# Products of v_m and w1 for four batches at once, kept in memory: an attention and mixture-of-experts kernel on one core

## The chip, the cores and the metric

The kernel runs on one core of one Trainium2 chip. The metric is the device time of one execution in microseconds; for the kernel before it is 1374.86 us, the median of 3 runs (1374.76 to 1375.8). A profile is one further execution, taken by the hardware profiler. In it the engines are PE (matmuls; PEld loads their weights), DVE (vector), ACT (scalar), POOL (GpSimd) and SP, which here only issues DMAs.

## The reference

Two parts, one behind the other, all in 32-bit floats. The first is an attention with 32 learned memory slots per head (8 batches, 8 heads, 576 positions, 64 per head); the second sends its result through four experts, weighted by given probabilities:

```python
a = softmax(phi, over positions)                    # 8 x 8 x 576 x 32
k_m, v_m = einsum(a, k), einsum(a, v)               # 32 slots of 64, per batch and head
attn = softmax(q @ k_m.T / 8, over the slots)
x = (attn @ v_m), heads side by side                # 4608 rows of 512
for e in range(4):
    h = maximum(x @ w1[e], 0.0)                     # 512 -> 1024
    out += p[:, e:e + 1] * (h @ w2[e])              # 1024 -> 512
```

## The kernel before

x is never formed. Since x = attn @ v_m, x @ w1 is attn @ (v_m @ w1): per batch, expert and half of the 1024 hidden columns the kernel makes a product of v_m and w1 ("vw": 2 tiles of 128 rows, 4 heads by 32 slots each, by 512 columns) and multiplies the transposed attention weights (AT) with it. 32-bit accuracy comes from pairs: a tile is split into a high part (a copy that rounds, on ACT) and a rest (a subtraction, on DVE or POOL), and PE does high x high, high x rest and rest x high.

**Tiling and order.** Batches go in four groups of two (odd is 0 or 1). A group has 4 experts, an expert 32 steps (STEPS), a group 128 (PAIR). Up to BEGIN, in the middle of group 1, the first stage runs step by step: `first` makes a tile of h, `second` multiplies it with w2 (lines 490 to 538). From BEGIN on the second stage runs in 80 units of 4 steps (`unit`, line 874); a unit does a block of h times w2 with seven block products (`product`, L819: a11, a12, t2, t3, t1, n4, a22) instead of eight, with operands that DVE, ACT and POOL make a unit ahead out of `rows` (L733 to L735). Four units are one block of weights; `load_part` (L682) fetches its 8 tiles (kw, plain w2, and v, precomputed sums of w2, both kept in memory), three of them in the first three units of the block before and five in its last, as buffers come free.

**What sets the order around the change.** The plan is a table written out by hand: `at(s, ...)` puts a piece of work at a step, and `run_plan` emits it where that step stands in the unit. All engines run their own instructions in order, SP its DMAs too: a DMA that waits for a buffer holds those behind it. ATT, VW_AT, VW_7, W1_AT, W1_7 and JOBS are those tables: when a batch's phi, k_m and v_m, scores and transposes are done, when a vw product is made, when w1 is loaded, when the sums of w2 are made and stored.

**vw in the kernel before.** `vw_mm` (L462) makes one product for one batch, expert and half: 8 matmuls with 64 rows by 32 columns against 512, each into its own 32 rows of two PSUM banks. `vw_out` copies the high part (ACT, L476) and subtracts (DVE, L477). The w1 tiles are loaded by `load_w1` (L166) into four buffers, which the matmuls free. In the second stage one of the four, and one of the five vw1 buffers, belongs to the ring of block weights. Only PSUM banks 0 and 1 are then free for the attention's and the vw's matmuls.

The prologue (lines 938 to 993) is written out by hand for batch 0; `keep_warm` (L935) is a run of matmuls without use.

Of the kernel before, what the change touches and what calls it, by code (L numbers as in the profile page):

```python
# [38 lines left out]

W1_AT = (15, 16, 17, 18)  # L40
VW_AT = (
    ((20, 23), (28, 33)),
    ((20, 23), (28, 32)),
    ((20, 23), (26, 31)),
    ((18, 28), (26, 33)),
    ((20, 23), (28, 30)),
    ((17, 20), (23, 26)),
)

ATT = {  # L50
    2: (22, 30, (93, 97, 102), (111, 112, 113)),
    3: (38, 46, (116, 118, 120), (PAIR + 2, PAIR + 4, PAIR + 6)),
    4: (88, 99, (PAIR + 66, PAIR + 76, PAIR + 84), (PAIR + 86, PAIR + 89, PAIR + 95)),
    5: (107, PAIR - 2, (PAIR + 102, PAIR + 108, PAIR + 115), (PAIR + 118, PAIR + 124, PAIR + 128)),
    6: (PAIR + 3, PAIR + 14, (2 * PAIR + 66, 2 * PAIR + 76, 2 * PAIR + 84), (2 * PAIR + 86, 2 * PAIR + 89, 2 * PAIR + 95)),
    7: (PAIR + 18, PAIR + 32, (2 * PAIR + 102, 2 * PAIR + 108, 2 * PAIR + 115), (2 * PAIR + 118, 2 * PAIR + 124, 2 * PAIR + 128)),
}

REST_0 = (2, 1, 6, 6, 1, 1, 5)
# [6 lines left out]
Q = 256  # L66
X_BANK, Y_BANK, AB_BANK = 4, 2, 6
JOBS = (
    (2, 0, 18, "Y", 5), (2, 1, 34, "Y", 5), (3, 0, 85, "Y", 5), (3, 1, 98, "Y", 5),
    (0, 0, PAIR + 2, "Y", 5), (0, 1, PAIR + 16, "Y", 5), (1, 0, PAIR + 30, "Y", 5),  # L70
    (1, 1, PAIR + 44, "Y", 5),
)
KEEP_AT, W2_AGAIN = (20, 12, -1, 20), 24
FIRST_LOADS = (-16, -7, -6, -5, -4, -3, -2, -1)
W1_7 = (6, 7, 22, 23)
VW_7 = (
    ((17, 34), (28, 36)),
    ((16, 35), (30, 38)),
    ((14, 30), (18, 34)),
    ((14, 30), (18, 38)),  # L80
    ((17, 34), (28, 36)),
    ((16, 35), (30, 38)),
    ((14, 30), (18, 34)),
    ((14, 30), (18, 34)),
    ((14, 30), (18, 34)),
)


@with_exitstack
def body(ctx: ExitStack, tc: tile.TileContext, qm, qt, kv, kvt, phi, prob, w1, w2, out):  # L90
# [238 lines left out]
    def kv_pick(b, gs=range(2), copy=nc.scalar.copy):  # L329
        src = st["kvp", b, gs[0]]  # L330
        n = 2 * len(gs)
        copy(
            kvm[b][:, 2 * gs[0]:2 * gs[0] + n].rearrange("p a j m -> p (a j m)"),
            src.rearrange("p g m -> p (g m)"),
        )
        give(src)
# [27 lines left out]

# [91 lines left out]
    def vw_mm(b, e, fh):  # L456

        ps = [bank("pm", 512) for _ in range(2)]
        for hp in range(NP):
            for j in range(2):  # L460
                r, m = v_half(j), slice(M * hp, M * hp + M)
                nc.tensor.matmul(  # L462
                    ps[j][m], kvm[b][r, hp, j], w1t[e, fh, hp // 2][r, hp % 2], start=True, stop=True
                )
# [8 lines left out]
    def vw_out(ps, b, e, fh, js=(0, 1)):  # L473
        for j in js:
            t = vw_tile(b // 2, e, b % 2, fh, j)
            nc.scalar.copy(t[:, 0, :], ps[j])  # L476
            nc.vector.tensor_sub(t[:, 1, :], ps[j], t[:, 0, :].bitcast(F32))  # L477
            give(ps[j])
# [85 lines left out]
    def at(s, unit):  # L564
        plan[s].append(unit if isinstance(unit, tuple) else (None, unit))
# [28 lines left out]
    def attention(b, s, turn, scores, turns):  # L594

        at(s, lambda: load_phi(b))
        at(turn, lambda: load_tail(b))
        for g in range(2):
            at(s + 3, lambda g=g: phi_max(b, g))
            at(s + 4, lambda g=g: phi_exp(b, g))  # L600
            at(s + 5, lambda g=g: phi_norm(b, g))
            at(turn + g, lambda g=g: phi_turn(b, g))
            at(turn + 1 + g, lambda g=g: phi_turn_out(b, g))
        at(turn + 2, lambda: phi_turn_tail(b))
        at(turn + 3, lambda: phi_turn_tail_out(b))
# [4 lines left out]
        at(turn + 12, lambda: kv_fold(b))  # L610
        at(turn + 13, lambda: kv_pick(b))
# [12 lines left out]
    for k in range(NG):  # L624
        for e in range(E):
# [69 lines left out]
    ph2 = {}  # L695

    def open_seven():
        two = lambda tag, n, *names: [
            att.tile([P, 2, 2, n], F32R, name=tag, tag=tag, bufs=2) for _ in range(2)
        ]  # L700
        ph2["Y"] = two("Y", Q)
        ph2["D"] = [
            t.rearrange("p s t (j c) -> p s t j c", j=2) for t in two("D", Q)
        ]
        ph2["N"] = two("N", P)
        for tag, n in ("g", 3), ("d", 2):
            ph2[tag] = att.tile([P, n, 2, P], F32, name=tag, tag=tag)
        ph2["n"] = att.tile([P, 2, P], F32, name="n", tag="n")
# [230 lines left out]
    with tc.manual_schedule():  # L939
# [27 lines left out]
        for g in range(2):
            for c2 in range(2):
                kv_mm(0, g, c2, raw["kv", 0, g, c2])
            kv_out(0, g)  # L970
            kv_fold(0, range(g, g + 1))
            kv_pick(0, range(g, g + 1), dve.tensor_copy)
# [12 lines left out]
        transposes_out(0, 0)
        keep_warm(4)
        for i in range(2):
            split_w2(0, 0, i, raw["w2", 0, 0], gps)
        for s in range(AHEAD):
            first(s)  # L990
# [12 lines left out]
    with tc.manual_schedule():  # L1003
# [59 lines left out]
```

## Time and profile before

| | |
|---|---|
| median of 3 runs | 1374.86 us |
| profiled execution, time | 1374.65 us |
| its span, first to last instruction | 1372.9 us |
| mean granted TensorE clock | 0.992 |
| PE busy | 1340.4 us (98%) |
| DVE, ACT, POOL busy | 769.5, 481.8, 396.6 us |
| DMA | 220.41 MB, mean 161 GB/s |
| second stage begins at | 568.6 us (its unit 0) |
| groups 2 and 3 begin at | 732.6 and 1061.0 us (units 16 and 48) |

How to read the rows. A group of instructions stands as line, engine, operation, what it writes <- what it reads, shapes and count, then busy time in us and mean ns of one, then idle time of the engine ahead of it and what ended that. A row of the waits is who waited <- for whom: us in total, times, longest us. A timeline row is start us, length us, then the instruction, with idle time ahead of it in brackets; neighbours of one kind are merged, and "SPq" is SP issuing. A matmul's length is longer than its distance to the next one, since they are pipelined: what a matmul costs PE is the distance from start to start.

### The profile page before, as it was taken

The numbers are of one execution on the slowest core, as the hardware profiler recorded it, in microseconds if no ns is written. First come the engines' busy times: TensorE is split into PE (matmuls) and PEld (weight loads), VectorE is DVE, ScalarE is ACT, GpSimd is POOL, SyncE is SP. The second block draws the span as 40 slices with busy tenths as digits, with TensorE's granted clock in tenths as the row PEclk, the third lists the DMA queues.
The fourth block names the chain that finished last, engine by engine and source line by source line (L and its number), as shares of the span: only waits on it lengthen the run. The fifth ranks groups of instructions, "written<-read, shape, count | busy, mean of one in ns | idle before, by whom it ended". The sixth has DMA issues, their size and how long they took to land.

```text
span 1372.9 us, 26361 instructions
## 1 busy us (share of the span) xinstructions
PE 1340.4 (98%) x10306; PEld 1170.6 (85%) x10306; DVE 769.5 (56%) x1798; ACT 481.8 (35%) x1215; POOL 396.6 (29%) x452
## 2 busy tenths in 40 slices
PE   7999999999999999999998999999999999999998
PEld 5687888878788787889887999988889899999998
DVE  4654423255343534566675666666666566666665
ACT  4433323243232332333333333333333333333332
POOL 1020304054002222243332333334343233333332
PEclk8999999999999999999999999999999999999999
DMA  8751827038565762633325533343522444443321
GB/s 307 254 200 62 301 93 262 32 119 300 185 235 203 250 213 86 215 112 114 143 102 208 188 119 120 116 151 112 200 93 97 188 154 154 154 154 133 127 94 72
DMA packets 64845, 220.41 MB, mean 161 GB/s; under 512 B 7249, under 2 KB 8401, under 8 KB 64721
## 3 DMA queue, kind: packets, MB, share of 16 engines
q1 hardware_dynamic: 55504, 185.17, 38.8%
q0 software_dynamic: 8064, 29.36, 5.4%
q10 hardware_dynamic: 1152, 4.19, 0.8%
q8 instruction: 81, 1.33, 0.4%
q14 instruction: 44, 0.35, 0.1%
HBM read 175.71 MB, written 42.99 MB: 159 GB/s over the span
## 4 chain that ended last, share of the span: by engine, by line
PE 93%; DVE 3%; DMA 2%; ACT 1%; issue 1%; SPq 0%; DVEq 0%; ACTq 0%
PE banks L819 29%; PE banks L534 7%; PE banks L535 7%; PE banks L536 7%; PE banks L733 6%; PE banks L735 6%; PE banks L734 6%; PE banks L462 5%; PE banks L501 4%; PE banks L502 4%; PE banks L503 4%; PE banks L857 1%; PE banks L858 1%; PE banks L859 1%; PE banks L307 1%; DVE vw L477 1%
## 5 line engine op out<-in xcount | busy, mean ns | idle before, releaser
L837 DVE SCALAR_TENSOR_TENSOR acc<-banks,pt,acc 128x256 f32<-128x256 f32 x528 | 252.1, 480 | 183.6 <-PE banks L819 182.1
L733 PE MATMUL banks<-AT,vw 128*128 128x256 f32 (+1 forms) x640 | 191.1, 299 | 0.0
L735 PE MATMUL banks<-AT,vw 128*128 128x256 f32 (+1 forms) x640 | 190.4, 298 | 0.0
L734 PE MATMUL banks<-AT,vw 128*128 128x256 f32 (+1 forms) x640 | 190.1, 297 | 0.0
L515 DVE SCALAR_TENSOR_TENSOR h<-banks,h 128x256 fp32r<-128x256 f32 x192 | 80.3, 420 | 170.7 <-ACT h L513 111.1
L800 POOL TENSOR_TENSOR D<-d,D 128x512 fp32r<-128x512 f32 x80 | 103.6, 1295 | 225.6 <-ACT D L799 162.7
L534 PE MATMUL banks<-w,h 128*128 128x512 f32 x384 | 151.3, 394 | 0.6 <-ACT h L513 0.6
L535 PE MATMUL banks<-w,h 128*128 128x512 f32 x384 | 150.9, 393 | 0.0
L536 PE MATMUL banks<-w,h 128*128 128x512 f32 x384 | 150.4, 392 | 0.0
L819 PE MATMUL banks<-w,Y 128*128 128x256 f32 x912 | 136.4, 284 | 7.0 <-DMA w<-kw 7.0
L513 ACT ACTIVATE h<-banks 128x256 fp32r<-128x256 f32 x192 | 73.4, 384 | 186.1 <-PE banks L503 157.2
L819 PEld LDWEIGHTS banks<-w,Y 128*128 128x128 f32 x912 | 123.6, 190 | 11.3 <-DMA w<-kw 3.9
L205 POOL TENSOR_TENSOR raw<-raw,sv 128x512 fp32r<-128x512 f32 x32 | 42.3, 1348 | 304.9 <-DVE raw L219 216.6
L819 PEld LDWEIGHTS banks<-w,D 128*128 128x128 f32 x768 | 104.5, 191 | 24.1 <-DVE acc L837 17.7
L819 PE MATMUL banks<-w,D 128*128 128x256 f32 x768 | 119.7, 288 | 4.5 <-DVE acc L837 4.5
L810 POOL TENSOR_TENSOR N<-n,N 128x256 fp32r<-128x256 f32 x80 | 59.2, 740 | 223.7 <-ACT N L809 110.3
L733 PEld LDWEIGHTS banks<-AT,vw 128*128 128x128 f32 x640 | 121.8, 190 | 2.2 <-DVE hm L748 0.4
L501 PE MATMUL banks<-AT,vw 128*128 128x320 f32 (+1 forms) x384 | 121.2, 316 | 1.8 <-DVE at L391 0.7
L734 PEld LDWEIGHTS banks<-AT,vw 128*128 128x128 f32 x640 | 121.3, 190 | 0.1
L735 PEld LDWEIGHTS banks<-AT,vw 128*128 128x128 f32 x640 | 120.9, 189 | 0.0
L785 ACT ACTIVATE Y<-banks 128x512 fp32r<-128x512 f32 x80 | 47.9, 598 | 190.7 <-DVE d L791 181.0
L502 PE MATMUL banks<-AT,vw 128*128 128x320 f32 (+1 forms) x384 | 113.8, 296 | 0.9 <-DVE zs L267 0.9
(132 smaller groups left out, 2613.7 us busy)
## 6 DMA issues: line engine op xcount, KB each, us to landing
w<-kw SPq DMA_DIRECT2D x92, 512.0 KB, 5.5
w<-v SPq DMA_DIRECT2D x68, 512.0 KB, 5.1
w<-in_w SPq DMA_DIRECT2D x64, 512.0 KB, 6.5
stage<-in_kv SPq DMA_DIRECT2D x32, 512.0 KB, 4.7
kw<-w POOLq DMA_DIRECT2D x24, 512.0 KB, 6.7
stage<-in_qm SPq DMA_DIRECT2D x16, 512.0 KB, 7.0
stage<-in_w SPq DMA_DIRECT2D x16, 512.0 KB, 4.5
raw<-in_w SPq DMA_DIRECT2D x16, 512.0 KB, 5.4
```

The lines of the kernel that those rows point to most:

```text
L501: nc.tensor.matmul(ps, w[:, 0, f], at_t[:, g, 0, c], start=g == 0, stop=False)
L502: nc.tensor.matmul(ps, w[:, 0, f], at_t[:, g, 1, c], start=False, stop=False)
L515: nc.vector.scalar_tensor_tensor(t[:, 1, to], ps[:, at_], 0.0, t[:, 0, to].bitcast(F32), ALU.max, ALU.subtract)
L534: nc.tensor.matmul(po[t], x[:, 0, :], w[:, 0, :], start=j == 0, stop=False)
L535: nc.tensor.matmul(po[t], x[:, 0, :], w[:, 1, :], start=False, stop=False)
L536: nc.tensor.matmul(po[t], x[:, 1, :], w[:, 0, :], start=False, stop=j == NJ - 1)
L733: nc.tensor.matmul(ps, w[:, 0, f], at_t[:, g, 0, c], start=g == 0, stop=False)
L734: nc.tensor.matmul(ps, w[:, 0, f], at_t[:, g, 1, c], start=False, stop=False)
L735: nc.tensor.matmul(ps, w[:, 1, f], at_t[:, g, 0, c], start=False, stop=g == 1)
L800: GP.tensor_sub(D[:, 1], d, D[:, 0].bitcast(F32))
L819: nc.tensor.matmul(ps, a[:, l, jj], w[:, r, c], start=start and jj + i == 0, stop=jj == 1 and i == 2, skip_group_check=True,)
L837: VE.scalar_tensor_tensor(a, src, p, a, ALU.mult, ALU.add)
```

## The change

- Groups 2 and 3 (batches 4 to 7) no longer use `vw_mm`. For them v_m is split on ACT and POOL (`v_split`) and put by small DMAs into one tile vs: per head the high part in rows 0 to 63, the rest in rows 64 to 127, the four batches side by side in 128 columns (`write_v`). `four_mm` multiplies it with a w1 tile in which a head's 64 rows stand twice (a new input, w1d): two matmuls per head, with w1's high part and its rest. One product holds the four batches' 32 slots of that head. `four_out` splits it on ACT and DVE into one of three buffers (vst), `to_memory` stores it by POOL's queue, and `load_vw` fetches for each batch the 32 rows per head that it needs, through SP's queue, in group 2 and again in group 3.
- The products stand in 32 units, from the last expert of group 1 to the third of group 2: two per unit. w1d comes through the staging buffers, which are loaded ahead in the order of the plan; its split uses ACT and POOL.
- The block operands share homes with tiles of the attention: one half of D with the tail of k and v (tag tl), N with phi (ph), g and d with the transposed phi (a), n with the small tiles xs, which then have two buffers left. Only six k_m/v_m tiles are kept instead of eight.
- Scores: batch 4's move into the first stage, batch 5's first to the start of the second; those of 6 and 7 go to the last quarter of group 2. k_m and v_m are ready one step earlier. The sums of w2 (JOBS) are made earlier.
- The prologue: warming matmuls are spread otherwise, both halves of batch 0's first vw product are made ahead of the first step, and its subtractions and the first split of w2 move.

```diff
-    4: (88, 99, (PAIR + 66, PAIR + 76, PAIR + 84), (PAIR + 86, PAIR + 89, PAIR + 95)),
+    4: (88, 99, (PAIR + 35, PAIR + 45, PAIR + 51), (PAIR + 43, PAIR + 53, PAIR + 59)),
...
-    (2, 0, 18, "Y", 5), (2, 1, 34, "Y", 5), (3, 0, 85, "Y", 5), (3, 1, 98, "Y", 5),
...
+    (2, 0, 18, "Y", 5), (2, 1, 34, "Y", 5), (3, 0, 58, "Y", 5), (3, 1, 72, "Y", 5),
...
-W1_7 = (6, 7, 22, 23)
-VW_7 = (
-    ((17, 34), (28, 36)),
...
+VW_7 = (6, 23), (17, 28)
+W1_7 = (-4, -3, 10, 18)
+FOUR_AT = ((0, 4, 8, 12), (16, 20, 24, 28))
+FOUR_LAG = 2
+VW_LOAD = ((21, 37), (26, 41))
...
-    kvm = [const.tile([P, NP, 2, M], F32, name=f"kvm{i}") for i in range(B)]
-    kvt_t = const.tile([P, H, P], F32, name="tail")
+    kvm = [const.tile([P, NP, 2, M], F32, name=f"kvm{i}") for i in range(6)]
+    kvt_t = att.tile([P, H, P], F32, name="tail", tag="tl")
...
+    def write_v(b):
+        if b == 4:
+            st["vs"] = att.tile([P, 2, NP, P], F32R, name="vs", tag="vs")
+        c = slice(M * (b - 4), M * (b - 4) + M)
+        for j in range(2):
+            for i in range(2):
+                nc.sync.dma_start(
+                    st["vs"][64 * i:64 * i + 64, j, :, c].bitcast(F32),
+                    st["vh", b][v_half(j), i].bitcast(F32),
+                )
+    def to_memory():
+        for key, t in done:
+            vwd[key] = dram.tile([P, 2, 512], F32, name="vwd" + "".join(map(str, key)))
+            nc.gpsimd.dma_start(vwd[key], t.bitcast(F32))
+        done.clear()
+    def four_split(raw, i):
+        w = wp.tile([P, 2, 512], F32R, name="w1", tag="w1", bufs=4)
+        split(w, raw[:, i, :], nc.gpsimd)
+        return w
+    def four_mm(h, w):
+        ps = bank("pm", 512)
+        for a in range(2):
+            nc.tensor.matmul(ps, st["vs"][:, h % 2, h // 2, :], w[:, a, :], start=a == 0, stop=a == 1)
+        return ps
+    def four_out(e, fh, h, ps):
+        t = att.tile([P, 2, 512], F32R, name="vst", tag="vst", bufs=3)
+        nc.scalar.copy(t[:, 0, :], ps)
+        nc.vector.tensor_sub(t[:, 1, :], ps, t[:, 0, :].bitcast(F32))
+        give(ps)
+        done.append(((e, fh, h), t))
+    def units_four(e, fh, hp):
...
+        out = [(0, (("w1d", e, fh, hp), load)), (2, other)]
+        for i in range(2):
+            h, x = 2 * hp + i, FOUR_LAG + 2 * i
+            out.append((x, lambda i=i, h=h: kept.update({2 + i: four_mm(h, kept[i])})))
+            out.append((x + 1, lambda i=i, h=h: four_out(e, fh, h, kept[2 + i])))
+            out.append((x + 2, to_memory))
+        return out
+    def load_vw(k, e, odd, fh):
+        c = slice(M * (2 * k + odd - 4), M * (2 * k + odd - 4) + M)
+        for j in range(2):
+            t = vw_tile(k, e, odd, fh, j)
+            for hp in range(NP):
+                nc.sync.dma_start(t[M * hp:M * hp + M].bitcast(F32), vwd[e, fh, 2 * hp + j][c])
...
+            if nk > 1:
+                for fh in range(2):
+                    for hp in range(NP if nk == 2 else 0):
+                        for i, u in units_four(ne, fh, hp):
+                            at(s + FOUR_AT[fh][hp] + i, u)
+                    for odd in range(2):
+                        at(s + VW_LOAD[odd][fh], lambda a=(nk, ne, odd, fh): load_vw(*a))
+                continue
...
         scores_mm(0, 0, raw["qm", 0, 0])
+        ps = vw_mm(0, 0, 0)
         scores_copy(0, 0)
         scores_turn(0, 0)
+        for j in range(2):
+            vw_high(ps, 0, 0, 0, j)
         scores_max(0, 0)
-        ps = vw_mm(0, 0, 0)
+        vw_rest(ps, 0, 0, 0, 0)
+        split_w2(0, 0, 0, raw["w2", 0, 0], gps)
         scores_exp(0, 0)
...
         transposes_out(0, 0)
-        keep_warm(4)
...
+        ps = vw_mm(0, 0, 1)
+        split_w2(0, 0, 1, raw["w2", 0, 0], gps)
+        first(0)
+        vw_out(ps, 0, 0, 1)
+        first(1)
         probabilities()
```

More of the change, by code (lines that the diff above doesn't have):

```diff
@@ L332, in kv_pick @@
         copy(
[L333 removed]
+            kvm[b % 6][:, 2 * gs[0]:2 * gs[0] + n].rearrange("p a j m -> p (a j m)"),
             src.rearrange("p g m -> p (g m)"),
@@ L360, in scores_mm @@
                 nc.tensor.matmul(
-                    sT[i][m, :nt * n], kvm[b][half, hp, i], q[half, hp, :nt * n],
+                    sT[i][m, :nt * n], kvm[b % 6][half, hp, i], q[half, hp, :nt * n],
                     start=True, stop=True,
@@ L462, in vw_mm @@
                 nc.tensor.matmul(
-                    ps[j][m], kvm[b][r, hp, j], w1t[e, fh, hp // 2][r, hp % 2], start=True, stop=True
+                    ps[j][m], kvm[b % 6][r, hp, j], w1t[e, fh, hp // 2][r, hp % 2], start=True, stop=True
                 )
@@ L471, in vw_tile, with vw_high, vw_rest @@
         return vw[key]
[L473 to L478, printed above, removed]
+    def vw_high(ps, b, e, fh, j):
+        nc.scalar.copy(vw_tile(b // 2, e, b % 2, fh, j)[:, 0, :], ps[j])
+    def vw_rest(ps, b, e, fh, j):
+        t = vw_tile(b // 2, e, b % 2, fh, j)
+        nc.vector.tensor_sub(t[:, 1, :], ps[j], t[:, 0, :].bitcast(F32))
+        give(ps[j])
@@ new lines, in vw_out, with v_split @@
+    def vw_out(ps, b, e, fh):
+        for j in range(2):
+            vw_high(ps, b, e, fh, j)
+            vw_rest(ps, b, e, fh, j)
+    vwd, done = {}, []
+    def v_split(b):
+        vh = att.tile([P, 2, NP, M], F32R, name="vh", tag="xs", bufs=3)
+        for j in range(2):
+            r = v_half(j)
+            split(vh[r], kvm[b % 6][r, :, j], nc.gpsimd)
+        st["vh", b] = vh
+    def write_v(b):
[8 more added lines that the diff above has]
+                )
@@ new lines, in four_out, with load, other @@
+    def four_out(e, fh, h, ps):
[5 more added lines that the diff above has]
+    def units_four(e, fh, hp):
+        kept = {}
+        def load(raw):
+            kept["raw"] = raw
+            kept[0] = four_split(raw, 0)
+        def other():
+            kept[1] = four_split(kept["raw"], 1)
+        out = [(0, (("w1d", e, fh, hp), load)), (2, other)]
[5 more added lines that the diff above has]
+        return out
@@ L637, in body @@
                 at(s + W2_AGAIN + j, lambda a=(nk, ne, j): load_w2(*a))
-            when = VW_7[(s - BEGIN) // STEPS] if s >= BEGIN else VW_AT[s // STEPS]
+            if nk > 1:
[6 more added lines that the diff above has]
+                continue
+            when, loads = (VW_7, W1_7) if s >= BEGIN else (VW_AT[s // STEPS], W1_AT)
             for fh in range(2):
                 for g in range(2):
-                    at(s + (W1_AT if s < BEGIN else W1_7)[2 * fh + g], lambda a=(ne, fh, g): load_w1(*a))
+                    at(s + loads[2 * fh + g], lambda a=(ne, fh, g): load_w1(*a))
                 for odd in range(2):
@@ L697, in open_seven, with half, open_last @@
     def open_seven():
[L698 to L708, printed above, removed]
+        def half(tag, bufs):
+            t = att.tile([P, 2, 2, Q], F32R, name="half", tag=tag, bufs=bufs)
+            return t
+        ph2["Y"] = [half("Y", 2) for _ in range(2)]
+        ph2["D"] = [half(tag, 1).rearrange("p s t (j c) -> p s t j c", j=2) for tag in ("tl", "D")]
+        N4 = att.tile([P, 2, 2, 2, P], F32R, name="n4", tag="ph")
+        ph2["N"] = [N4[:, i] for i in range(2)]
+        g = att.tile([P, 5, 2, P], F32, name="g", tag="a")
+        ph2["g"], ph2["d"] = g[:, :3], g[:, 3:]
+    def open_last():
+        n = att.tile([P, 2 * P], F32, name="xs", tag="xs", bufs=3)
+        ph2["n"] = n.rearrange("p (j c) -> p j c", j=2)
     def open_ring():
@@ L966, in body @@
             phi_norm(0, g)
[L967 to L972, printed above, removed]
+        kvr = lambda g, c2: kv_mm(0, g, c2, raw["kv", 0, g, c2])
+        one = lambda g: range(g, g + 1)
+        kvr(0, 0)
+        keep_warm(6)
+        kvr(0, 1)
+        kv_out(0, 0)
+        kvr(1, 0)
+        kv_fold(0, one(0))
+        kv_pick(0, one(0), dve.tensor_copy)
+        kvr(1, 1)
+        kv_out(0, 1)
+        keep_warm(2)
+        kv_fold(0, one(1))
+        kv_pick(0, one(1), dve.tensor_copy)
+        keep_warm(2)
         scores_mm(0, 0, raw["qm", 0, 0])
+        ps = vw_mm(0, 0, 0)
         scores_copy(0, 0)
         scores_turn(0, 0)
+        for j in range(2):
+            vw_high(ps, 0, 0, 0, j)
         scores_max(0, 0)
-        ps = vw_mm(0, 0, 0)
+        vw_rest(ps, 0, 0, 0, 0)
+        split_w2(0, 0, 0, raw["w2", 0, 0], gps)
         scores_exp(0, 0)
+        keep_warm(8)
         soft_sum(0, 0)
-        vw_out(ps, 0, 0, 0, (0,))
         soft_scale(0, 0, dve)
-        keep_warm(3)
         transposes(0, 0)
-        vw_out(ps, 0, 0, 0, (1,))
+        vw_rest(ps, 0, 0, 0, 1)
         transposes_out(0, 0)
-        keep_warm(4)
[L987 to L990, printed above, removed]
+        ps = vw_mm(0, 0, 1)
[3 more added lines that the diff above has]
+        first(1)
         probabilities()
```

45 lines of the change are left out of this document (21 added, 24 removed).

## The prediction, made before the changed kernel had run

> **What bounds the kernel now.** I read the page first, then the groups by line, the waits, a table of windows, and the timeline at the places that these point to. The page's shares, and its chain of work that ended last:
>
> ```profile
> PE 1340.4 (98%) x10306; PEld 1170.6 (85%) x10306; DVE 769.5 (56%) x1798; ACT 481.8 (35%) x1215; POOL 396.6 (29%) x452
> PE 93%; DVE 3%; DMA 2%; ACT 1%; issue 1%; SPq 0%; DVEq 0%; ACTq 0%
> ```
>
> The reader is to see one engine, PE, in nearly all of the time, so an edit is worth what it takes from PE's own stream plus the waits inside that stream. Windows tell where PE waits (columns: length, then busy time and count of PE, PEld, DVE, ACT and POOL, granted clock, share of the DMA engines, GB/s):
>
> ```profile
> 0.00:25.00 25.00, 17.33 (x160) 11.47 (x161) 8.20 (x20) 6.77 (x14) 1.64 (x8) 0.80 0.94 313
> 322.00:332.00 10.00, 10.00 (x119) 8.56 (x111) 3.64 (x13) 3.65 (x12) 7.47 (x8) 1.00 0.99 324
> 332.00:342.00 10.00, 10.00 (x58) 8.87 (x58) 4.94 (x14) 4.52 (x15) 3.89 (x7) 1.00 1.00 392
> 732.60:779.40 46.80, 42.59 (x327) 38.05 (x325) 26.09 (x60) 15.03 (x35) 13.97 (x16) 0.93 0.55 206
> 779.40:817.90 38.50, 38.50 (x310) 35.73 (x309) 25.05 (x58) 13.91 (x32) 14.05 (x16) 1.00 0.41 138
> 1061.00:1107.10 46.10, 42.01 (x326) 37.58 (x325) 26.07 (x60) 14.98 (x35) 13.99 (x16) 0.96 0.55 209
> ```
>
> The last three are blocks of four units of the second stage: 779.4 to 817.9 is an undisturbed one; 732.6 and 1061.0 are where groups 2 and 3 begin. These two are 8.3 and 7.6 us longer and run at a granted clock of 0.93 and 0.96. PE's waits of any size name the same two places and, less, DVE:
>
> ```profile
> PE banks L819 <- DMA w<-kw: 8.1, 6, 1.9
> PE banks L819 <- DVE acc L837: 7.5, 9, 1.5
> ```
>
> SP's timeline ahead of the first of them shows why those weights were late:
>
> ```profile
> 702.03 1.95 SPq L844 DMA_DIRECT2D out<-acc  x2
> 704.02 23.93 SPq L166 DMA_DIRECT2D w<-in_w  x2
> 728.01 0.43 SPq L682 DMA_DIRECT2D w<-kw  x1
> 733.68 0.47 SPq L682 DMA_DIRECT2D w<-kw  x1
> ...
> 737.36 0.98 PE L819 MATMUL banks<-w,Y 128*128 128x256 f32 x3 [1.78 <-DMA w<-kw]
> 739.81 1.01 PE L819 MATMUL banks<-w,Y 128*128 128x256 f32 x3 [1.48 <-DMA w<-kw]
> ```
>
> The pair of w1 loads sits on SP from 704.02 to 727.95: the second waits for a w1 buffer, which the old products (L462) hold. The weights kw01 to kw03 of the next block stand behind it and are issued only from 728.01 on, for a block that begins at 732.6.
>
> **The old products.** One of them in the undisturbed block, with its neighbours, and the group that holds all:
>
> ```profile
> 809.85 0.87 PE L819 MATMUL banks<-w,Y 128*128 128x256 f32 x6
> 810.56 0.28 PE L733 MATMUL banks<-AT,vw 128*128 128x256 f32 x1
> ...
> 811.27 0.87 PE L819 MATMUL banks<-w,D 128*128 128x256 f32 x6
> 812.07 1.09 PE L462 MATMUL banks<-w,kvm 64*32 64x512 f32 x16
> 813.09 0.98 PE L819 MATMUL banks<-w,D 128*128 128x256 f32 x6
> 813.91 0.31 PE L733 MATMUL banks<-AT,vw 128*128 128x320 f32 x1
> ...
> L462 PE MATMUL banks<-w,kvm 64*32 64x512 f32 x1024 | 73.4, 608 | 0.0
> ```
>
> Six block products take 0.71 us when left alone (809.85 to 810.56). From 811.27 to 813.91 are two such sixes and one old product: 2.64 - 2 x 0.71 = 1.22 us for it, its change of shape on both sides included. 1024 records at 16 each are 64 products; groups 2 and 3 have 4 batches x 4 experts x 2 halves = 32. Removed: 32 x 1.22 = 39.0 us, all on PE's path.
>
> **The four-batch products** are 8 heads x 8 halves x 2 matmuls = 128, 128 by 128 against 512 columns. Matmuls of that form follow each other in the first stage like this:
>
> ```profile
> 31.38 0.39 PE L536 MATMUL banks<-w,h 128*128 128x512 f32 x1
> 31.61 0.39 PE L534 MATMUL banks<-w,h 128*128 128x512 f32 x1
> 31.84 0.39 PE L535 MATMUL banks<-w,h 128*128 128x512 f32 x1
> 32.06 0.39 PE L536 MATMUL banks<-w,h 128*128 128x512 f32 x1
> ```
>
> That is 0.227 us from start to start (0.68 / 3), and their shape is that of their neighbours, so I add nothing around them: 128 x 0.227 = 29.1 us. Net of the exchange: -9.9 us. [...]
>
> **SP's queue at the start of group 2.** Before, in program order (kw00 to kw03 are the next block's first weights, w1 the inputs of the old products, acc the results):
>
> ```order
> L682 DMA w2_5432<-kw00_980 128x1024
> L844 DMA out<-acc_4004 128x512 x2
> L166 DMA w1_6993<-in_w1 128x1024
> L166 DMA w1_7027<-in_w1 128x1024
> L682 DMA w2_5318<-kw01_1008 128x1024
> L844 DMA out<-acc_4183 128x512 x2
> ```
>
> Now, between the same two rows (stage is a staging buffer of inputs, vwd a product kept in memory):
>
> ```order
> L760 DMA w2_5574<-kw00_987 128x1024
> L924 DMA out<-acc_4067 128x512 x2
> L139 DMA stage_7085<-in_w1d 128x1024
> L546 DMA vw_7113<-vwd000_6602 32x1024
> L546 DMA vw_7113<-vwd002_6719 32x1024
> L546 DMA vw_7113<-vwd004_6845 32x1024
> L546 DMA vw_7113<-vwd006_6962 32x1024
> L546 DMA vw_7118<-vwd001_6660 32x1024
> L546 DMA vw_7118<-vwd003_6781 32x1024
> L546 DMA vw_7118<-vwd005_6903 32x1024
> L546 DMA vw_7118<-vwd007_7020 32x1024
> L760 DMA w2_5460<-kw01_1015 128x1024
> ```
>
> The two loads that waited for L462 are gone; in their place kw01 stands behind one staged load and eight loads of 128 KB. The last of these waits until vwd007 is stored: its store is planned 3 steps ahead, and a step is a quarter of a unit, 38.5 / 16 = 2.4 us, so 7.2 us. The nearest rows for the store and for a weight load, then POOL's own price of a store and of a split:
>
> ```profile
> w<-kw SPq DMA_DIRECT2D x92, 512.0 KB, 5.5
> kw<-w POOLq DMA_DIRECT2D x24, 512.0 KB, 6.7
> L178 POOL DMA_DIRECT2D kw<-w x24 | 13.3, 557 | 4.4 <-issue 4.4
> L162 POOL TENSOR_TENSOR w<-stage,w 128x512 fp32r<-128x512 f32 x18 | 24.4, 1399 | 71.2 <-ACT w L161 71.1
> L800 POOL TENSOR_TENSOR D<-d,D 128x512 fp32r<-128x512 f32 x80 | 103.6, 1295 | 225.6 <-ACT D L799 162.7
> ```
>
> At 6.7 us the store lands about when SP comes to it. Were SP held 5 us there, kw01 would still have over two units (some 19 us) to land in 5.5. So I let both long blocks shrink to the undisturbed length. Each of them holds 48 records of L462, one old product more than the undisturbed one: 46.8 - 38.5 - 1.2 = 7.1 and 46.1 - 38.5 - 1.2 = 6.4. Gain: 13.5 us, clock loss included; bounds 0 (a new queue holds the weights as long) and 13.5.
>
> **What the second stage takes on.** POOL in one unit of the stage with the products, now (half and n are the block operands D and N, vst the product on its way to memory):
>
> ```order
> L504 DMA vwd301_9663<-vst_9637 128x1024
> L154 TENSOR_TENSOR w_9665<-stage,w_9665 128x512
> L880 TENSOR_TENSOR half<-g,half 128x512
> L890 TENSOR_TENSOR n_5481<-xs,n_5481 128x256
> L504 DMA vwd_9722<-vst 128x1024
> L154 TENSOR_TENSOR w_9728<-stage,w_9728 128x512
> L857 TENSOR_TENSOR a_9745<-g,a_9745 128x256
> L860 TENSOR_TENSOR t_9746<-g,t_9746 128x256
> ```
>
> Before, the four subtractions stood alone, 14.05 us in the undisturbed block of four units, 3.5 a unit. Two splits at 1.40 and two stores at 0.56 raise that to 7.4 us, of a unit of (38.5 - 2 x 1.22 + 16 x 0.227) / 4 = 9.9 us. It fits, but subtractions that PE waits for now stand behind a store that waits for DVE. The block operands are made three to four steps (7 to 10 us) ahead of their use, which covers a lag of a few us; the splits only two steps (4.9 us). ACT gets four copies a unit where it had one, DVE two subtractions where it had one (0.68 us). DMA: a block of four units moves 8 weights, 4 staged loads, 8 stores and 16 small loads, 24 times 512 KB = 12.6 MB in 39.7 us, 317 GB/s, where it was 138. The two windows of 324 and 392 GB/s at a share of 0.99 and 1.00 are what the engines gave: 81 to 97% taken. Five of a block's eight weights are issued in its last unit with some 8 us to spare, and 5.5 us will grow. I put 4 us on all of this (0.5 per block of the eight with products); bounds 0 and 16 (2 per block). Group 3 only loads and loses its old products, so nothing is added there.
>
> **Scores and homes.** Batch 4's scores leave the second stage, where DVE makes PE wait (7.5 us in 9 waits), for the first stage; batches 6 and 7 are squeezed into the last quarter of group 2, with DVE also there. PE's share of scores is only moved. I take -1; bounds -4 and +3. The shared homes (tail with D, phi with N, a with g and d) are taken when batch 7's last use is past, some 10 steps earlier, so 0. The 16 small copies of v (32 KB each) and the splits ahead of them lie in the first stage; by the rows of SP above one DMA takes it 0.4 to 0.5 us to issue, 8 us at most over four batches, and PE waits for none of them before group 2: 0, at worst +2 if SP brings something else late.
>
> **Prologue.** PE's stream around the first step:
>
> ```profile
> 24.32 0.66 PE L438 MATMUL banks<-ident,at 128*128 128x128 f32 x4 [1.22 <-DVE at L411]
> 25.65 0.38 PE L501 MATMUL banks<-AT,vw 128*128 128x256 f32 x1
> 25.96 1.04 PE L462 MATMUL banks<-w,kvm 64*32 64x512 f32 x2
> 28.43 1.08 PE L462 MATMUL banks<-w,kvm 64*32 64x512 f32 x14
> 30.93 0.39 PE L534 MATMUL banks<-w,h 128*128 128x512 f32 x1
> ```
>
> Now the second half's product stands ahead of L501, in the time in which AT was copied; 1 us of it is hidden, and the vw subtraction of 0.68 us leaves the chain ahead of L438. Warming matmuls fill other gaps. Up to 3 us; but the loads that follow run at a DMA share of 0.94, so I take -2, bounds 0 and -3.
>
> **Sum** against the profiled execution's own time of 1374.65 us (span 1372.9 and 1.75 around it; the median of the runs is 1374.86, which changes nothing): 1374.65 - 39.0 + 29.1 - 13.5 - 1 - 2 + 4 = 1352.3, say 1352 us. With every bound at its good end 1344.
>
> **The rivals.** *Weights stay late.* Eight small loads and a store's landing hold SP as the w1 loads did, or the products' traffic makes the block starts wait; against it stands the lead of two units. Then the 13.5 stay: 1366. *In-order queues stretch each unit.* ACT's copy of a product needs one of three vst buffers, free when a store has landed; two a unit make 1.5 units, 14.8 us, for a step of 2.4, POOL's 0.6 and 6.7 to land. It decides when a store takes over 11.8 us, or POOL lags over 5; a wait of 0.5 us for half of 64 products costs 16: 1364 with the 4 taken out. *The DMA engines become the bound*, on the other side. It decides for PE below 317 GB/s, and for a total slower than before below 12.6 MB / (39.7 + 3.3) = 293, since 8 x 3.3 eats the 26.4 of the sum without the 4. No row shows loads into 32 partitions; at an assumed 280 a block takes 45.0 us, 5.3 more: 1348 + 8 x 5.3 = 1390. For it stands the 324 row, against it the 392. [...] *It doesn't do what it says*: the diff leaves no L462 for batches 4 to 7, so no chance.
>
> **Chances.** Forecast (1344 to 1359) 0.58; weights late or queues (1359 to 1372) 0.27; DMA bound 0.15, of which 0.09 is slower, 0.04 within 0.2% and 0.02 faster. 0.2% is 2.7 us, about what a measurement of this kernel can tell from no change. Faster 0.87, same 0.04, slower 0.09. Range 1343 to 1368: it takes in the good end and the first two rivals' prices, and leaves out the DMA bound.
>
> **What would show it.** Right: no wait of PE on weights at the starts of groups 2 and 3 and a clock of 1.0; undisturbed blocks of 39.7 us with products and 36.1 in group 3; 128 matmuls 0.227 apart. Wrong: blocks in group 2 well over 40 us with a DMA share near 1, waits of PE on w or of ACT on vst, or weights that land 10 us and more after issue.

## The result, and the profile after

The changed kernel takes 1340.3 us (median of 4 runs, 1338.0 to 1341.3), the kernel before 1375.0 us beside it: a ratio of 0.9744, 95% interval 0.9727 to 0.9761. The gain is 34.7 us where 22.6 were forecast, and the time lies below the range of 1343 to 1368. The profiled execution took 1340.53 us, its span is 1338.7. In runs 1, 5 and 6 below one execution of four took far longer (3324.9, 1820.3 and 1822.9 us) and is not in their ratios. From the page after: the engines, what the DMA engines moved in 40 equal slices, and the chain that ended last.

```profile
PE 1318.9 (99%) x9940; PEld 1182.4 (88%) x9940; DVE 772.0 (58%) x1798; ACT 517.2 (39%) x1287; POOL 512.9 (38%) x588
GB/s 321 229 228 62 221 170 172 293 79 242 262 279 171 166 217 122 111 126 158 153 251 338 341 339 326 319 325 310 307 233 187 263 162 187 178 166 179 175 167 72
PE 95%; DMA 3%; DVE 1%; ACT 0%; issue 0%; SPq 0%; ACTq 0%; DVEq 0%
```

PE is the bound as before. The three rows at the top of its waits, all engines' names as before (L899 is the block product, L917 the addition into the results):

```profile
PE banks L371 <- ACT sT L362: 3.0, 1, 3.0
PE banks L430 <- DVE at L403: 2.5, 1, 2.5
PE banks L899 <- DVE acc L917: 2.2, 4, 1.1
```

The 8.1 us for late weights are gone from this list, and the 7.5 us for DVE's additions have become 2.2. Four blocks of four units by windows: the first of group 2, an undisturbed one with products, the first of group 3, an undisturbed one there.

```profile
737.30:776.60 39.30, 39.30 (x294) 38.09 (x293) 27.18 (x62) 19.74 (x45) 27.68 (x33) 1.00 0.97 344
815.80:855.00 39.20, 39.20 (x293) 37.98 (x292) 27.20 (x62) 19.99 (x45) 28.15 (x33) 1.00 0.94 324
1053.60:1089.60 36.00, 36.00 (x281) 35.29 (x280) 23.80 (x57) 12.10 (x30) 14.56 (x18) 1.00 0.62 185
1160.70:1196.30 35.60, 35.60 (x279) 35.10 (x278) 23.11 (x53) 11.98 (x29) 14.06 (x17) 1.00 0.60 178
```

The first block of a group is now as long as its neighbours, at a clock of 1.0. The blocks with products do take up 0.94 to 0.97 of the DMA engines' time, and PE is busy for all of each window nevertheless. SP ahead of group 2, where the pair of w1 loads had stood for 24 us:

```profile
717.19 6.40 SPq L546 DMA_DIRECT2D vw<-vwd  x8
724.19 0.36 SPq L952 DMA_DIRECT2D out<-accm  x1
724.64 0.38 SPq L760 DMA_DIRECT2D w<-kw  x1
725.99 1.50 SPq L924 DMA_DIRECT2D out<-acc  x2
727.58 0.42 SPq L139 DMA_DIRECT2D stage<-in_w1d  x1
728.09 0.40 SPq L760 DMA_DIRECT2D w<-kw  x1
728.58 4.14 SPq L760 DMA_DIRECT2D w<-v  x2
```

Eight small loads hold SP 6.4 us, and the next weight follows at 724.64, for a block that begins at 737.3.

**Where the time went.** The second stage runs from its unit 0 to the end of the span: 1372.9 - 568.6 = 804.3 us before, 1338.7 - 574.5 = 764.2 after, 40.1 less. The first stage is 5.9 longer in the two profiled executions. The experiments take both apart.

### The profile page after: what moved, and what is told of

Read it like the earlier page. It is cut to its first block, busy times and chain, and to the rows that moved or that the text cites. A ratio compares the mean times of both kernels' runs of the same rounds, so it can differ in the third digit from the quotient of the medians.

```text
span 1338.7 us, 26561 instructions
## 1 busy us (share of the span) xinstructions
PE 1318.9 (99%) x9940; PEld 1182.4 (88%) x9940; DVE 772.0 (58%) x1798; ACT 517.2 (39%) x1287; POOL 512.9 (38%) x588
## 2 busy tenths in 40 slices
DMA packets 90704, 288.08 MB, mean 215 GB/s; under 512 B 16720, under 2 KB 17872, under 8 KB 90576
## 4 chain that ended last, share of the span: by engine, by line
PE 95%; DMA 3%; DVE 1%; ACT 0%; issue 0%; SPq 0%; ACTq 0%; DVEq 0%
PE banks L899 30%; PE banks L602 7%; PE banks L603 7%; PE banks L604 7%; PE banks L813 6%; PE banks L815 6%; PE banks L814 6%; PE banks L569 4%; PE banks L571 4%; PE banks L570 4%; PE banks L454 2%; PE banks L515 2%; DMA stage<-in_w 1%; PE banks L938 1%; PE banks L937 1%; PE banks L939 1%
## 5 line engine op out<-in xcount | busy, mean ns | idle before, releaser
L917 DVE SCALAR_TENSOR_TENSOR acc<-banks,pt,acc 128x256 f32<-128x256 f32 x528 | 253.2, 480 | 143.0 <-PE banks L899 139.0
L899 PE MATMUL banks<-w,half 128*128 128x256 f32 x1680 | 250.3, 282 | 0.9 <-DVE acc L917 0.9
L899 PEld LDWEIGHTS banks<-w,half 128*128 128x128 f32 x1680 | 227.1, 189 | 8.4 <-DVE acc L917 1.6
L154 POOL TENSOR_TENSOR w<-stage,w 128x512 fp32r<-128x512 f32 x82 | 107.9, 1324 | 118.3 <-ACT w L153 117.6
L880 POOL TENSOR_TENSOR half<-g,half 128x512 fp32r<-128x512 f32 x80 | 103.1, 1289 | 121.9 <-ACT half L879 79.8
L569 PE MATMUL banks<-AT,vw 128*128 128x320 f32 (+1 forms) x384 | 122.3, 318 | 2.7 <-DVE h L583 2.0
L571 PE MATMUL banks<-AT,vw 128*128 128x320 f32 (+1 forms) x384 | 114.6, 299 | 0.0
L570 PE MATMUL banks<-AT,vw 128*128 128x320 f32 (+1 forms) x384 | 114.4, 298 | 0.1
L865 ACT ACTIVATE half<-banks 128x512 fp32r<-128x512 f32 x80 | 47.8, 598 | 171.2 <-DVE g L871 140.7
L890 POOL TENSOR_TENSOR n<-xs,n 128x256 fp32r<-128x256 f32 x80 | 59.1, 739 | 141.3 <-ACT n L889 77.2
```

The lines of the kernel that those rows point to most:

```text
L154: eng.tensor_sub(dst[:, 1, :], raw, dst[:, 0, :].bitcast(F32))
L569: nc.tensor.matmul(ps, w[:, 0, f], at_t[:, g, 0, c], start=g == 0, stop=False)
L570: nc.tensor.matmul(ps, w[:, 0, f], at_t[:, g, 1, c], start=False, stop=False)
L571: nc.tensor.matmul(ps, w[:, 1, f], at_t[:, g, 0, c], start=False, stop=g == 1)
L899: nc.tensor.matmul(ps, a[:, l, jj], w[:, r, c], start=start and jj + i == 0, stop=jj == 1 and i == 2, skip_group_check=True,)
L917: VE.scalar_tensor_tensor(a, src, p, a, ALU.mult, ALU.add)
```

## The experiments

Each time below is the ratio to the kernel before in the same runs, and that ratio times the kernel before.

**1 and 2. What does an old product cost?** By the undisturbed blocks it isn't 1.22 us: 38.50 before, with two of them, against 35.60 in group 3 after, with none, is 1.45 each. So the old shape goes back into group 3, four to a pass. The results aren't used, and the operands are others.

```diff
+    def again(s):
+        if s < 3 * PAIR or (s - 3 * PAIR) % STEPS not in (14, 18, 30, 2):
+            return
...
+        for hp in range(NP):
+            for j in range(2):
+                r, m = v_half(j), slice(M * hp, M * hp + M)
+                nc.tensor.matmul(
+                    ps[j][m], kvm[0][r, hp, j], vw[3, e, odd, fh, hp // 2][r, hp % 2].bitcast(F32),
+                    start=True, stop=True,
+                )
```

> The changed kernel with 16 matmul groups of the old shape (8 matmuls of 64 rows by 32 columns against 512, in plain f32) put back into group 3, four to a pass at its steps 2, 14, 18 and 30, with old operands whose result nobody reads: no copy and no subtraction after them, so PE alone pays. If an old product costs PE 1.22 us, as the prediction took from one pair of neighbours, the time is 1340.3 + 16 x 1.22 = 1359.8, and undisturbed blocks of group 3 grow from 35.56 to 38.0. If it costs 1.47 us, as the blocks of before less those of after say, and PE alone pays it, 1363.8 and blocks of 38.5. If 0.2 to 0.25 us of the 1.47 were the copy on ACT and the subtraction on DVE, this run shows 1.25 a product and the next one 1.47.

The second adds what had followed an old product:

```diff
+        for j in range(2):
+            t = att.tile([P, 2, 512], F32R, name="vst", tag="vst", bufs=3)
+            nc.scalar.copy(t[:, 0, :], ps[j])
+            nc.vector.tensor_sub(t[:, 1, :], ps[j], t[:, 0, :].bitcast(F32))
```

> As the run before, with the two copies on ACT and the two subtractions on DVE behind each of the 16, into a buffer that nobody reads. PE alone pays: the same time as the run before within 1.5 us. ACT and DVE pay a part: 3 to 4 us more than it, 16 x 0.2 to 0.25.

Measured: 0.9890 (0.9862 to 0.9917), 1360.0 us, and 0.9937 (0.9915 to 0.9959), 1366.5 us. A block of group 3 in the first, then in the second:

```profile
1166.50:1204.50 38.00, 38.00 (x311) 35.55 (x310) 23.11 (x53) 11.97 (x29) 14.04 (x17) 1.00 0.60 170
```

```profile
1172.30:1210.70 38.40, 38.40 (x310) 35.65 (x309) 25.32 (x57) 14.13 (x33) 14.01 (x17) 1.00 0.59 167
```

(38.0 - 35.6) / 2 = 1.20 us for the matmuls alone, (38.4 - 35.6) / 2 = 1.40 with their output. So PE's own price was read rightly, and 0.2 us of it lay elsewhere. (The totals differ by 6.5, more than 16 x 0.2 = 3.2: the second stage of the two profiled executions began at 572.8 and 577.8 us, though the first stage of both kernels is the same; of this more under the prologue.) Where the 0.2 lies is seen when DVE and PE are laid side by side, 7 us into a unit, in the run with output:

```profile
1139.76 1.29 DVE L1011 TENSOR_TENSOR vst<-banks,vst 128x512 fp32r<-128x512 f32 x2 [1.18 <-ACT vst L1010]
1140.97 0.47 DVE L917 SCALAR_TENSOR_TENSOR acc<-banks,pt,acc 128x256 f32<-128x256 f32 x1
...
1141.04 0.51 PE L899 MATMUL banks<-w,t 128*128 128x256 f32 x3
1141.50 0.97 PE L899 MATMUL banks<-w,n 128*128 128x256 f32 x6
1142.31 0.31 PE L813 MATMUL banks<-AT,vw 128*128 128x320 f32 x1
```

and at the same place without:

```profile
1134.54 0.48 DVE L917 SCALAR_TENSOR_TENSOR acc<-banks,pt,acc 128x256 f32<-128x256 f32 x1 [1.42 <-PE banks L899]
...
1135.57 0.52 PE L899 MATMUL banks<-w,t 128*128 128x256 f32 x3
1135.92 0.88 PE L899 MATMUL banks<-w,n 128*128 128x256 f32 x6
1136.64 0.31 PE L813 MATMUL banks<-AT,vw 128*128 128x320 f32 x1
```

Without output the n4 product starts 0.35 us after t1's last three matmuls start and takes 0.72 to the next rows (1135.92 to 1136.64). With it, it starts after 0.46 and takes 0.81: it writes into a PSUM bank that DVE's addition L917 has to read out first (to 1141.44, 0.06 us ahead of n4), and that addition stands behind the two subtractions. It is a wait too short for the list of waits, and it stands three block products behind the old product.

**3. The hold on SP alone.** The kernel before with the second pair of w1 loads issued when its buffer is free, ahead of groups 2 and 3 only.

```diff
+                    late = 9 * fh - g * fh if nk > k and k else 0
-                    at(s + (W1_AT if s < BEGIN else W1_7)[2 * fh + g], lambda a=(ne, fh, g): load_w1(*a))
+                    at(s + (W1_AT if s < BEGIN else W1_7)[2 * fh + g] + late, lambda a=(ne, fh, g): load_w1(*a))
```

> The kernel before with one thing changed: in the two passes ahead of groups 2 and 3 the second pair of w1 loads is issued at step 31 instead of 22 and 23, when the buffer it needs is free, so that it does not hold SP. All old products stay. If the hold on SP made the two long blocks, both shrink from 46.8 and 46.1 to about 39.7 (38.5 and one product) and the time is 1374.9 - 13.5 = 1361.4, with no wait of PE on kw there. Rival: the weights are late because their buffers come free late or the DMA engines are busy there; then the blocks stay above 44 and the time above 1371.

Measured: 0.9905 (0.9879 to 0.9931), 1362.1 us. The two blocks that had taken 46.8 and 46.1, and an undisturbed one between them:

```profile
735.50:775.40 39.90, 39.79 (x325) 35.95 (x324) 25.80 (x60) 14.99 (x35) 14.03 (x16) 1.00 0.48 169
775.40:813.90 38.50, 38.50 (x310) 35.73 (x308) 25.05 (x58) 13.91 (x32) 14.05 (x16) 1.00 0.39 138
1057.00:1097.10 40.10, 39.99 (x326) 36.00 (x325) 25.89 (x60) 15.04 (x35) 14.01 (x16) 1.00 0.49 168
```

6.9 + 6.0 = 12.9 us, and the waits on kw are gone. The rival falls. Over a third of the change's gain thus needed no new products, only a pair of DMAs in another place.

**4. The tables alone.** The kernel before with the changed rows 4 and 5 of ATT, JOBS and VW_AT, as the diff of the change has them.

> The kernel before with only the changed tables of the attention of batches 4 and 5, of the sums of w2 and of the first stage's products (ATT rows 4 and 5, JOBS, VW_AT): batch 4's scores leave the second stage for the first, batch 5's stand at its start. All old products and the hold on SP stay. Theory from the blocks: of the 40.1 us that the second stage lost, some 9 belong to neither the products nor the two long blocks, 3 of them only moved (the first stage gains them) and 6 waits of PE on DVE; so here the second stage shrinks by 8 to 9 and the total by about 6, to 1369. Rival, as predicted: the scores are only moved, 1373 to 1375; then the waits on DVE went because the old products' subtractions went.

Measured: 0.9994 (0.9982 to 1.0006), 1374.0 us. For the total my theory falls and the prediction's value stands. The starts of the units tell more: units 0 to 15 take 158.2 us in place of 164.0, 5.8 less, and the others 2.1 more, 1.6 of it in the two long blocks. So the second stage takes 1369.3 - 568.7 = 800.6 us, 3.7 less than before. The first stage pays for it: its steps 160 to 184, where batch 4's scores now lie, take 68.8 us in place of 65.8. (It ends where it ended before all the same, since step 8 began 3.7 us earlier in this execution.) The waits on DVE change little in sum:

```profile
PE banks L818 <- DMA w<-kw: 8.8, 6, 2.3
PE banks L818 <- DVE acc L836: 6.0, 8, 1.5
```

6.0 us here, 7.5 before, 2.2 after. All nine of before stand in blocks with scores, and seven of them end 5.5 to 6.7 us after an old product began. One of these in the kernel before, on DVE, then PE (L477 are the product's subtractions, L404 the first of the sums of the scores' softmax, L837 the addition):

```profile
1023.33 1.29 DVE L477 TENSOR_TENSOR vw<-banks,vw 128x512 fp32r<-128x512 f32 x2 [0.49 <-ACT vw L476]
1024.54 0.68 DVE L404 TENSOR_REDUCE guarded<-at 128x16 f32<-128x512 f32 x1
...
1025.64 0.39 DVE L837 SCALAR_TENSOR_TENSOR acc<-banks,pt,acc 128x256 f32<-128x256 f32 x1
...
1026.08 0.98 PE L819 MATMUL banks<-w,D 128*128 128x256 f32 x6 [1.52 <-DVE acc L837]
```

The old product's subtractions and the scores' sums stand together ahead of the addition that PE waits for, in the way seen in run 2. In units 16 to 79, where this run moves no scores, such waits are 4.3 us before and in this run, and 0.2 after. But the change also moves the scores of batches 6 and 7 there (rows 6 and 7 of ATT), which no run does alone, so how much of these 4.1 us is due to the subtractions is argued, not shown.

**5 and 6. How near were the limits that the rivals named?** The changed kernel with one more transfer from memory to memory a unit of group 2:

```diff
+        if 16 <= u < 48:
+            for _ in range(1):
+                d = dram.tile([P, 2, DM], F32, name=f"more{u}")
+                nc.sync.dma_start(d, kept_for["w2", 0, 0])
```

> The changed kernel with one more transfer of 512 KB from memory to memory in each of the 32 units of group 2, issued by SP; nobody reads its result. A block of four units then moves 14.7 MB in place of 12.6. If the 310 to 341 GB/s of the slices of group 2 is what the engines can give, the blocks grow from 39.2 to 14.7 / 0.341 = 43.1 us and the time by 8 x 3.9 = 31, to 1371. If it is only what is asked for, and the 392 of the first stage's window can be had, 375 GB/s fit and PE hardly waits: 1340 to 1345.

Measured: 0.9796 (0.9766 to 0.9826), 1346.8 us, 6.5 more than the changed kernel. The trace, of which only the bytes are used, has 304.86 MB in place of 288.08, the 16.8 MB that were added. The expectation counts eight full blocks, but the last two of group 2 have no products, so six move 14.7 MB. A limit of 341 GB/s would have cost 6 x 3.9 = 23 us; if the six bear all of the 6.5, it is 1.1 us each, and 14.7 MB in 39.2 + 1.1 us are some 365 GB/s, an estimate. So the share of 0.94 to 0.97 in the blocks after was no sign that the engines were used up.

And the changed kernel with two vst buffers:

```diff
-        t = att.tile([P, 2, 512], F32R, name="vst", tag="vst", bufs=3)
+        t = att.tile([P, 2, 512], F32R, name="vst", tag="vst", bufs=2)
```

> The changed kernel with two buffers instead of three for the products on their way to memory. ACT's copy of a product then waits for the store of the product before the last: one unit, 9.1 to 11.5 us, for 2.4 (copy to store), 0.6 (issue) and 6.6 (landing), 9.6 in all. If stores land in 6.6 us in the median and few take longer, PE hardly feels it: 1340 to 1343. If the in-order queues were near their limit, as the rival of the prediction had it, ACT stands 0.5 to 2 us in half of the units and PE behind it: 1348 to 1365.

Measured: 0.9836 (0.9802 to 0.9871), 1352.3 us, 12 more. From ACT's waits, which had no such row with three buffers:

```profile
ACT vst L520 <- DMA vwd<-vst: 24.7, 22, 2.6
```

So the rival of the in-order queues was a real one: ACT stands 22 times, units 16 to 47 take 323.8 us in place of 316.3, and the third buffer is what keeps PE from it. My first guess (no cost) was wrong: the 9.6 us that a store needs, 6.6 for its landing included, don't fit into units of 9.1 and 9.4 us.

**7 and 8. The prologue.** The changed kernel with the prologue of before (its text from the kernel before, nothing else), and the kernel before with the new one:

> The changed kernel with the prologue of before: the order of the work up to the first step, the warming matmuls, and batch 0's second half product at step 0. Theory from the step times of the first stage: the new prologue begins the first step 3.1 us earlier and then loses about 6 in waits between 28 and 62 us, a net loss of some 2.9, so the time is 1340.3 - 2.9 = 1337.4 and the step that begins at 62 us is 2 to 4 us earlier. Rival, as predicted: the new prologue is worth 2 to 3 us, and the loss up to 62 us belongs to the tables of the first stage, which stay: 1342 to 1343.

> The kernel before with the new prologue alone. The run before it, with the prologue put back, showed no difference beyond the 2 us by which step 8 moves from one execution to the next. Theory: what the first step gains (3 us) is lost by step 8, since the loads of the first 60 us end then whatever the order, so step 8 begins between 57 and 64 us and the time is within 2 us of 1374.9. Rival: it is worth 2 us as predicted, 1373 or less.

Measured: 0.9752 (0.9729 to 0.9774), 1341.0 us: no difference from the changed kernel; and 1.0055 (1.0038 to 1.0072), 1382.4 us: alone it costs 7.5, nearly all of it by step 8, which begins at 63.8 us in place of 56.9. Neither the 2.9 us nor the 2 fits. What happens at step 6 of the changed kernel, on DVE, then PE in the same time, then two windows:

```profile
47.81 0.42 DVE L583 SCALAR_TENSOR_TENSOR h<-banks,h 128x256 fp32r<-128x256 f32 x1 [1.52 <-ACT h L581]
50.77 0.75 DVE L245 TENSOR_REDUCE nm<-ph 128x1 f32<-128x576 f32 x1 [2.53 <-DMA ph<-in_phi]
52.54 0.75 DVE L245 TENSOR_REDUCE nm<-ph 128x1 f32<-128x576 f32 x1 [0.84 <-DMA ph<-in_phi]
53.21 0.41 DVE L583 SCALAR_TENSOR_TENSOR h<-banks,h 128x256 fp32r<-128x256 f32 x1
...
53.77 0.60 PE L569 MATMUL banks<-AT,vw 128*128 128x320 f32 x1 [2.02 <-DVE h L583]
54.17 0.63 PE L603 MATMUL banks<-w,h 128*128 128x512 f32 x1
54.60 0.63 PE L604 MATMUL banks<-w,h 128*128 128x512 f32 x1
```

```profile
50.00:54.00 4.00, 1.98 (x44) 1.48 (x43) 2.36 (x5) 1.73 (x5) 0.00 (x0) 0.96 0.99 303
54.00:60.00 6.00, 6.00 (x31) 5.09 (x35) 2.23 (x10) 1.75 (x6) 0.00 (x0) 0.74 0.49 167
```

The first steps of the program are put in order by a scheduler. It moved the maximum over batch 2's phi (L245) from step 25 up to step 6, where DVE stands for phi's load; the subtraction of h stands behind it, PE waits 2.0 us for that, and the granted clock falls, to 0.66 from 53.5 to 54.0 us and 0.50 from 54.0 to 57.0: matmuls of 512 columns 0.43 us apart (54.17 to 54.60). The kernel before has the same hold, 2.9 us of DVE, but no fall of the clock (1.00 in both windows); with the new prologue in it the hold is 4.58. The changed kernel with the old prologue waits there too, 2.1 and 1.0 us on PE, its clock is 0.50 from 54 to 60 us, and its step 8 begins at 62.3 us where the new prologue's begins at 62.0: what the new one gained is gone by then.

**9 to 11. Three versions without that hold.**

```diff
-        if b == 1:
+        if b in (1, 2):
             tc.keep_in_program_order(i)
```

> The changed kernel with the maximum over phi of batch 2 kept at its planned step 25, as batch 1's is, where the scheduler had moved it up to step 6. There DVE stood from 48.2 to 50.8 and 51.7 to 52.5 us for phi's load, the subtraction of h behind it, PE behind that for 2.0 us, and the granted clock fell to 0.74 from 54 to 60 us. Theory: the wait and the slow clock go, step 8 begins 3 to 5 us earlier and the time is 1335 to 1337.5. Rival: another load is late there and PE waits as long for it: 1339 to 1341.

> As the run before, with the prologue of before as well. Theory: with the wait at step 6 gone, nothing takes back what a prologue gains or loses; the new one begins step 0 3 us earlier and waits 3 us for ACT at 31, so the two stand within 2 us of each other, 1334 to 1338. Rival: the new prologue is worth the 2 us of the prediction once step 6 doesn't hide it: 2 us or more above the run before.

The third also takes the third of the four pairs of w2 tiles later:

```diff
-REST_0 = (2, 1, 6, 6, 1, 1, 5)
+REST_0 = (2, 1, 6, 6, 1, 3, 5)
```

> As the first of these three, with the third pair of w2 tiles of batch 0's expert taken at step 3 instead of 1. In the changed kernel ACT stood from 31.2 to 33.8 us for that load, the copy of the scores behind it, and PE behind that for 3.0 us. Theory: this wait goes too and the time is 2 to 3 us below the first of these three. Rival: the load or the scores of the next batch are late at the next place: the same time within 1 us.

Measured: 0.9724 (0.9704 to 0.9744), 1336.7 us; 0.9737 (0.9719 to 0.9755), 1338.5 us; 0.9706 (0.9688 to 0.9724), 1334.3 us. The two windows from 50 to 60 us again, in the first of them:

```profile
50.00:54.00 4.00, 4.00 (x26) 3.57 (x22) 0.72 (x3) 1.35 (x5) 0.00 (x0) 1.00 1.01 368
54.00:60.00 6.00, 6.00 (x77) 4.27 (x75) 2.43 (x6) 1.25 (x5) 0.00 (x0) 1.00 0.73 234
```

PE is busy throughout at a clock of 1.0, and step 8 begins at 57.0 us in place of 62.0. The time falls by about 3, in intervals that overlap (0.9727 to 0.9761 for the changed kernel). With the old prologue it is the same within the intervals, so the new prologue by itself is worth nothing that these runs can tell. What it had won is lost at 31 us, where ACT stands for a w2 load with the scores' copy behind it, in the changed kernel:

```profile
33.75 0.62 ACT L153 CAST w<-stage 128x512 fp32r<-128x512 f32 x1 [2.60 <-DMA stage<-in_w]
34.28 0.32 ACT L362 COPY sT<-banks 128x64 f32<-128x64 f32 x2
```

and in the last version:

```profile
31.06 0.61 ACT L153 CAST w<-stage 128x512 fp32r<-128x512 f32 x1
31.79 0.33 ACT L362 COPY sT<-banks 128x64 f32<-128x64 f32 x2
```

The wait on PE was 3.0 us, from 31.5 to 34.5, and the clock fell there as well, to 0.50 from 33.2 us on. The 6.8 us from there in the changed kernel, then in the last version:

```profile
33.20:40.00 6.80, 5.46 (x30) 3.51 (x31) 3.73 (x11) 3.40 (x10) 0.00 (x0) 0.50 0.54 184
33.20:40.00 6.80, 6.80 (x54) 5.36 (x54) 5.92 (x18) 4.71 (x12) 0.00 (x0) 1.00 0.76 246
```

The last version measures 2.4 us less than the first of the three, in intervals that overlap, and 6 less than the changed kernel: the fastest of all here.

## Why the prediction was right or wrong

| Term | forecast | measured | from |
|---|---|---|---|
| 32 old products | -39.0 | -46.4 | 32 x 1.45, blocks |
| 128 new matmuls | +29.1 | +28.8 | 8 x (39.2 - 35.6), blocks |
| two long blocks | -13.5 | -12.9 | run 3 |
| scores, units 0 to 15 | } -1 | -5.5 | unit starts; run 4 has -5.8 |
| waits on DVE, units 16 to 79 | } | -4.1 | rest; the waits' list has 4.1 |
| new stalls | +4 | 0 | blocks, waits |
| first stage, scores and prologue | -2 | +5.9 | the two profiled executions |
| sum on 1374.65 | 1352.3 | 1340.5 | the rest closes it; 1340.53 measured |

The -5.5 is 162.8 - 164.0 for these units, less 7.2 for two blocks of new products and plus 2.9 for two old ones. The sum missed by 11.8 us: 7.4 from the old products, 8.6 from scores and waits on DVE, 4.0 from stalls and 0.3 from the new matmuls, against 7.9 from the first stage and 0.6 from the long blocks. That it missed by no more is in part luck, since the loss in the first stage offset a part of the gains that it had left out.

**The old products: the size of the term failed.** "2.64 - 2 x 0.71 = 1.22 us for it, its change of shape on both sides included" is right for PE's stream, as run 1 shows. It left out the output of an old product, two copies on ACT and two subtractions of 0.68 us on DVE, which I entered only as what DVE takes on, never as what PE is freed from. In undisturbed blocks this is 0.2 to 0.25 us a product, 7.4 us in all, of which run 2 shows 0.20 a product. In blocks with scores it is up to 4.1 more, together with the scores' own work on DVE. The sum gave this term no bounds, so its good end of 1344 could not hold what came. They should have been worked out from whole units with a product and without; units 75 to 79 of the kernel before have none and could have been read: unit 75 takes 8.21 us where unit 71 takes 9.47, unit 76 takes 8.55 where unit 72 takes 9.94.

**The new matmuls: right**, 28.8 / 128 = 0.225 us each, where the rows before gave 0.227.

**The long blocks: right**, place, cause and size.

**New stalls: "I put 4 us on all of this" was 4 too many**, and its caution about the share of the DMA engines was the wrong one. The queues were the nearer limit, as run 6 shows with its 12 us; the DMA bound, given 0.15, needed engines that give less than 317 GB/s, and by the estimate from run 5 they gave some 365. The 280 GB/s and 45.0 us a block of that rival were assumed, and no run shows them: with its 16 loads into 32 partitions the block takes 39.2 us, at 324 GB/s.

**Scores: nearly right in sum, not in the parts.** Run 4 has -0.9 (interval -2.5 to +0.8) for batches 4 and 5, with the long blocks still there. In the changed kernel units 0 to 15 save 5.5 and the first stage pays some 2.7 for it (step 160 begins 3.0 us later than before, step 184 5.7): -2.8, inside the bounds. The 4.1 us of waits are the part of "7.5 us in 9 waits" that the prediction named and left with the scores.

**Prologue: wrong sign of what mattered.** "Up to 3 us; but the loads that follow run at a DMA share of 0.94" saw the danger and put no price on it; it is worth 0 in this kernel and loses 7.5 in the kernel before. Of the 5.9 us in the first stage, what the scores don't explain arises ahead of step 16, at the waits at 31 and 51 us. These differ even among kernels whose first stage is the same: in the changed one and in runs 1 and 2 they are 2.7 to 4.2 and 1.9 to 3.6 us, and unit 0 begins at 572.8 to 577.8 us. Why is not known.

## What to carry to other kernels

An operation's price is what its whole block loses when it goes, its outputs on the other engines included: read it from a block with it and one without (1.45 us here), and only then from its neighbours on PE (1.22). When in-order queues feed PE, look for what stands behind a wait, and first for a DMA or a reduction that could simply be issued later: here two such moves are worth 13 and about 3 us. A DMA share of 0.94 to 0.97 was no bound here: 2.1 MB more in each block of group 2 cost 6.5 us in all (run 5). Ask what more traffic costs.

## What the runs showed of the hardware

- The DMA engines stood at a share of 0.91 to 1.03 in the changed kernel (four windows of 20 us between 740 and 880 us, 325 to 352 GB/s); with 2.1 MB more in each block the time grew by 6.5 us, about 1 us a block if the six full ones bear it (run 5).
- A wait of PE of 2.0 us at 51.7 us in the changed kernel was followed by 3 us of matmuls at half rate, 0.43 us apart in place of 0.23, at a granted clock of 0.50 (54.0 to 57.0 us); waits of 0.5 and 0.9 us at the same place before were not (1.00 from 49 to 60 us). In the same execution of the changed kernel, with a wait of 3.0 us at 31.5 us, the granted clock was 0.50 from 33.2 to 40.0 us; after a wait of 2.5 us at 21.3 us it was 1.00 (24 to 31 us).
- A store of 512 KB landed 6.6 us after issue in the median of the 64 stores of products; with two buffers in place of three ACT stood 22 times for one, 24.7 us in all (run 6).
- In the profiled execution of run 4 the granted clock reads 0.95 from 62 to 733 us, where it is 1.00 in the kernel before; its span is 1369.3 us, the kernel before's 1372.9.
